# Attention inside a feed-forward pass: units of attention taken in pairs per visit to the tensor engine, PSUM banks dealt out anew, global scores in one piece, one order list for the whole program

## The chip, the cores and the metric

The kernel runs on one core of one Trainium2 chip. The metric is the device time of one execution, in microseconds; the median of three runs of the kernel before is 951.62 (951.41 to 951.68). Engines are named as in the profile: PE is the tensor engine's matmul, PEld its weight load, DVE the vector engine, ACT the scalar engine, POOL GpSimd, and SP the queue that issues most DMAs.

## The reference

Local and global attention feed a layer norm and a feed-forward network; float32 throughout.

```python
# q_l, k_l, v_l: (8 batches, 8 heads, 512, 64); q_g, k_g, v_g: (8, 8, 32, 64)
s_g = scale * q_g @ concat(k_g, k_l).T            # 32 global rows see all 544 keys
out_g = softmax(s_g) @ concat(v_g, v_l)
s_ll = where(|i - j| <= 32, scale * q_l @ k_l.T, -1e9)
s_l = concat(scale * q_l @ k_g.T, s_ll)           # a local row sees 32 global keys and a window
out_l = softmax(s_l) @ concat(v_g, v_l)
x = concat(out_g, out_l)  -> (8, 544, 512)        # heads side by side
xn = (x - mean) / sqrt(var + 1e-6) * g_ln
out = x + relu(xn @ w_ch1) @ w_ch2                # 512 -> 2048 -> 512
```

## The kernel before

**Feed-forward network.** The 4,352 rows are cut into nine chunks: eight local ones (c0 to c7) of four row tiles (512 rows) and a global one (c8) of two. A chunk runs through 16 column blocks f of the hidden layer. `Ffn.first` (L643) makes 12 matmuls of 128x512 into one PSUM bank, `ph`: the low part of the weight times the high part of x, high times low, high times high, four of each. `high` (L656) writes `hh`, the rectified block, with ACT; `low` (L662) writes `hl`, the remainder, with DVE. `second` (L669) makes three matmuls for each row tile into the banks `acc0` to `acc3`. The order on PE is first(f+1), then second(f), so that ACT and DVE have the time of second(f-1) and first(f+1) to make hh and hl of f. There are two `ph` banks (`ps_h`, `bufs=2`), which alternate.

**Attention.** The next chunk's attention is made between these matmuls, in visits of PE to it. A local unit (`Local`, L310) is 256 rows of two heads: `score` (L334) makes 16 matmuls on 64x32 tiles, 128 columns each, into halves of two banks; DVE's `lowest` (L357, four pairs of instructions) scales, masks and takes the row extreme; ACT's `exp` (L370) follows four times; `transposes` (L396) makes 16 DVE transposes into `pt` (for the first 16 units PE transposes them, `turn`, L387); `sums` (L404) makes 16 matmuls on 128x32 tiles, 64 columns each, in the free half of a score bank; `scale` (L427) writes x. There are 64 local units, eight of them ahead of the first chunk's network. The other 56 have a visit each (`visit`, L806), which scores one unit and sums the one before it.

A global unit (L550) is four batches' 32 global rows of two heads: scores in two halves of 272 columns (`score_global`, L470), in two visits, then eight PE transposes (`transpose_global`, L512, in a third), then in the next unit's second visit 40 matmuls of sums (`value_global`, L523), 32 of them in the 128x32 tiling and 8 for the last 32 keys in a 32x32 one. There are eight, all in c7. Their keys `gk` and values `gv` have one buffer each, so a unit's keys are loaded when the scores of the unit before are done (L579), and its values when that unit's sums are.

**What sets the order.** PSUM has eight banks: four `acc`, two `ph`, two `att` (taken in turn for scores, sums and transposes). The first chunk and all ahead of it are ordered by `Plan` (L53): operations with an engine, an estimated cost, a key and what they wait for, given out one by one to the engine that can begin soonest, and, among those that can begin there, the lowest key. In the first chunk the weights are also split into high and low parts (`Split`, L206), by DVE and ACT. From c1 on the order is that in which `ffn` (L694) and `visit` are written, and the constants `PLACES` (L32) say between which matmul groups the visits lie. Each engine executes its instructions in that order.

Of the kernel before, what the change touches and what calls it, by code (L numbers as in the profile page):

```python
# [19 lines left out]
P = 128  # L20
# [11 lines left out]
PLACES = {7: (1, 3.4), 9: (0, 3.5)}  # L32
# [14 lines left out]
SPREAD = 10.0  # L47
# [5 lines left out]
class Plan:  # L53
# [13 lines left out]
    def emit(self):  # L67
        free = dict.fromkeys(self.waiting, 0.0)
        wire, landed = 0.0, []
        while self.count:  # L70
            best = None
            for e, ops in self.waiting.items():
                can = [(max(free[e], t), o) for o in ops if (t := o.ready()) is not None]
                if not can:
                    continue
                if e == "SP" and len(landed) >= IN_FLIGHT:
                    can = [(max(t, landed[-IN_FLIGHT]), o) for t, o in can]
                first = min(t for t, _ in can) + PATIENCE
                t, _, o = min(
                    ((t, o.key, o) for t, o in can if t <= first), key=lambda x: (x[1], x[0])  # L80
                )
                if best is None or t < best[0]:
                    best = t, e, o
            t, e, o = best
            self.waiting[e].remove(o)
            self.count -= 1
            free[e] = o.end = t + o.cost
            if o.size:
                wire = max(wire, o.end) + o.size / WIRE
                landed.append(wire + LANDING)  # L90
                o.late = landed[-1] - o.end
            o.run()


class Operation:
    def __init__(self, engine, cost, key, run, after, behind, late, size):
        self.engine, self.cost, self.key, self.run = engine, cost, key, run
        self.after = [a for x in after for a in (x if isinstance(x, (list, tuple)) else [x]) if a]
        self.behind, self.late, self.size, self.end = behind, late, size, None

    def ready(self):
        t = 0.0
        if self.behind:
            if self.behind.end is None:
                return None
            t = self.behind.end
        for a in self.after:
            if a.end is None:
                return None
# [5 lines left out]
def attention_ffn_kernel(  # L115
# [15 lines left out]
    SA = gk.shape[4]  # L131
# [14 lines left out]
    ps_h = ctx.enter_context(tc.tile_pool(name="ps_h", bufs=2, space=bass.MemoryType.PSUM))  # L146
    ps_a = ctx.enter_context(tc.tile_pool(name="ps_a", bufs=2, space=bass.MemoryType.PSUM))
# [137 lines left out]
    def norm(x, js):  # L285

        n = Norm(x, js)
        for j in js:
            n.stats(j)
        for j in js:  # L290
            n.join(j)
        n.root()
        n.shift()

        def apply():
            for j in js:
                n.apply(j)
                yield

        return apply()  # L300

    def att(name):
        return ps_a.tile([P, 512], F32, name=name, tag="att")
# [6 lines left out]
    class Local:  # L310


        def __init__(self, b, hp, half, alone, on_pe):
# [3 lines left out]
            self.next = None  # L317

        def load(self, part=None):

            if part != 1:
                if self.alone:
                    shape, tag = [P, 2 * (KT * P + DM)], UNITS[units.index(self)]
                    u = wpool.tile(shape, F32, name="u", tag=tag)
                else:
                    u = self.ap.tile([P, eu.shape[4]], F32, name="u", bufs=2)
                self.u = u
                self.e = u[:, :21 * WIN]
                self.v = u[:, 21 * WIN:eu.shape[4]].rearrange("p (w d) -> p w d", w=8)
            ends = (0, 21 * WIN, eu.shape[4])  # L330
            c0, c1 = ends[::2] if part is None else ends[part:part + 2]
            nc.sync.dma_start(self.u[:, c0:c1], eu[self.at][:, c0:c1])

        def score(self, banks):  # L334
            self.mn = small.tile([P, 4], F32, name="mn")
            self.sm = small.tile([P, 4], F32, name="sm")
            self.p = self.ap.tile([P, 4, P], F32, name="p", bufs=3)
            sc = self.sc = [bank("sc") for bank in banks]
            self.free = sc[1][:, 2 * P:]
# [40 lines left out]
        def scores(self):  # L380
            self.score([att, att])
            yield
            for c in range(4):
                self.lowest(c)
                self.exp(c)

        def turn(self, bank):  # L387
            self.tp = bank("tp")
# [7 lines left out]
        def transposes(self):  # L396
            self.pt = self.ap.tile([P, 4, P], F32, name="pt", bufs=2)
            for g in range(4):
                gp = slice(g * WIN, (g + 1) * WIN)
                for r in range(4):  # L400
                    rp = slice(r * WIN, (r + 1) * WIN)
                    nc.vector.transpose(out=self.pt[rp, :, gp], in_=self.p[gp, :, rp])  # L402
# [17 lines left out]
        def total(self):  # L420
            self.ri = small.tile([P, 4], F32, name="ri")
# [14 lines left out]
        def values(self, pv=None):  # L436
            self.sums(att("pv") if pv is None else pv)
            self.total()
            self.inverse()
            self.scale()  # L440
            if self.next and self.next.next:
                self.next.next.load()

# [5 lines left out]
        def finish(self):  # L449
            if self.at[1] == HP - 1:  # L450
                for j in range(2):
                    self.store(j)
                return norm(self.x, range(2))
            return ()

    def load_global_keys(ap, bg, hp):
        kr = ap.tile([P, BG, SA], F32, name="gk")
        qr = ap.tile([P, BG, SG], F32, name="gq", bufs=2)
        nc.sync.dma_start(qr, gq[bg, hp])
        nc.sync.dma_start(kr, gk[bg, hp])  # L460
        return qr, kr

    def load_global_values(ap, bg, hp):
        vr = ap.tile([P, BG, 4, P], F32, name="gv")
        vt = ap.tile([P, P], F32, name="gvt")
        nc.sync.dma_start(vr, gv[bg, hp])
        nc.sync.dma_start(vt, gt[bg, hp])
        return vr, vt

    def score_global(ap, qr, kr, out):  # L470
        p = ap.tile([P, 2, SA], F32, name="gp")
        mn = small.tile([P, 4], F32, name="mn")
        sm = small.tile([P, 4], F32, name="sm")
        for part in range(2):
            c0, c1 = part * SA // 2, (part + 1) * SA // 2
            sc = [ps_a.tile([P, 512], F32, name="sc", tag="att") for _ in range(2)]
            out[:] = p, sm, sc[1][:, c1 - c0:]
            for i in range(BG):
                for h in range(2):
                    nc.tensor.matmul(  # L480
                        sc[h][i * SG:(i + 1) * SG, :c1 - c0],
                        qr[h * D:(h + 1) * D, i, :],
                        kr[h * D:(h + 1) * D, i, c0:c1],
# [5 lines left out]
            yield  # L489
            for h in range(2):  # L490
                nc.vector.tensor_scalar(
                    p[:, h, c0:c1],
                    sc[h][:, :c1 - c0],
                    -QSCALE,
                    BIG if part == 0 else mn[:, 2 * h:2 * h + 1],
                    ALU.mult,
                    ALU.min,
                    accum_out=mn[:, 2 * h + part:2 * h + part + 1],
                )
            if part == 0:  # L500
                yield
        for h in range(2):
            nc.scalar.activation(
                p[:, h, :],
                p[:, h, :],
                AF.Exp,
                bias=mn[:, 2 * h + 1:2 * h + 2],
                scale=-1.0,
                accum_out=sm[:, h:h + 1],
            )  # L510

    def transpose_global(ap, p):  # L512
        pt = ap.tile([P, 2, 4, P], F32, name="gpt")
        tail = ap.tile([P, 2, SG], F32, name="gpt_tail")
        for h in range(2):
            t0 = ps_a.tile([P, 512], F32, name="t0", tag="att")
            for c in range(4):
                nc.tensor.transpose(t0[:, c * P:(c + 1) * P], p[:, h, c * P:(c + 1) * P], ident)  # L518
            nc.vector.transpose(out=tail[:, h, :], in_=p[:, h, 512:SA])
            nc.scalar.copy(pt[:, h], t0.rearrange("p (c q) -> p c q", c=4))  # L520
        return pt, tail

    def value_global(hp, pt, tail, vr, vt, sm, x, pv):  # L523
        if pv is None:
            pv = ps_a.tile([P, 512], F32, name="pv", tag="att")
        for h, cs in enumerate(((0, 1, 2, 3, 4), (4, 0, 1, 2, 3))):
            hd = slice(h * D, (h + 1) * D)
            for c in cs:
                for i in range(BG):
# [751 lines left out]
```

## Time and profile before

| | us |
|---|---|
| median of 3 runs | 951.62 (951.41 to 951.68) |
| profiled execution | 950.43 |
| its span in the trace | 948.6 |
| outside the span | 1.8 |
| PE busy | 919.4 (97%) |
| DVE busy | 573.2 (60%) |
| ACT busy | 316.8 (33%) |

PE is busy for nearly the whole span, and the chain of work that ended last runs on PE for 87% of it; PE's idle time is 29 us in all, and most of it lies ahead of the first chunk's network. The busy share is a mean over stages, so what a piece of work takes is read from the stage it lies in. The rows further down give stages and pieces: a local chunk's network with the next chunk's attention in it takes 103 us, and c7 with the global attention 128.

### The profile page before, as it was taken

To read this page: it belongs to the slowest core of one execution; us is meant where nothing else is said; L and a number is where in the kernel's file an instruction comes from. 1 tells how busy PE (TensorE), PEld (TensorE's weight loads), DVE (VectorE), ACT (ScalarE), POOL (GpSimd) and SP (SyncE) were. 2 spreads that over 40 slices of the span, in tenths; PEclk is the share of its full clock that TensorE was granted. 3 is DMA by queue.
4 is the path that set the end of the run, shared out by engine and by line. 5 is a ranking of instruction groups with operands and counts; after the bars stand their busy time and mean duration, and the time that the engine had idled before them with its cause. 6 is when DMAs were issued, how large, how long until landed. Compare 5 with 4: busy or idle time off the path is not lost.

```text
span 948.6 us, 21082 instructions
## 1 busy us (share of the span) xinstructions
PE 919.4 (97%) x8616; PEld 716.0 (75%) x8616; DVE 573.2 (60%) x1885; ACT 316.8 (33%) x842; POOL 48.4 (5%) x150
## 2 busy tenths in 40 slices
PE   5699999999999999999999999999999999999997
PEld 3477777777777787777777777778777777777896
DVE  4799987766577647766776647664776442222311
ACT  5788843232223222322323232223232123222210
POOL 4111010000000000000000000000000000000000
PEclk9699999999999999999999999999999999999999
DMA  8766643324223223323332422323322425353300
GB/s 355 286 247 234 221 168 118 97 75 141 82 75 97 79 99 119 103 95 114 119 96 75 139 84 75 97 75 104 120 97 74 164 95 196 114 191 145 101 23 23
DMA packets 31873, 118.81 MB, mean 125 GB/s; under 512 B 4256, under 2 KB 6304, under 8 KB 27680
## 3 DMA queue, kind: packets, MB, share of 16 engines
q1 hardware_dynamic: 31776, 117.46, 35.7%
q8 instruction: 68, 1.11, 0.5%
q14 instruction: 29, 0.24, 0.1%
HBM read 99.62 MB, written 17.83 MB: 124 GB/s over the span
## 4 chain that ended last, share of the span: by engine, by line
PE 87%; DVE 5%; DMA 2%; issue 2%; ACT 2%; POOL 1%; SPq 0%; ACTq 0%; POOLq 0%; DVEq 0%
PE acc L676 40%; PE ph L651 36%; PE sc L347 3%; DVE pt L402 3%; PE sc L410 3%; DMA gk<-in_gk 2%; PE t L610 2%; PE sc L531 1%; ACT p L371 1%; PE sc L480 1%; PE tp L390 1%; DVE ob L688 1%; PE t L518 0%; POOL mask L184 0%; DVE hl L664 0%
## 5 line engine op out<-in xcount | busy, mean ns | idle before, releaser
L676 PE MATMUL acc<-w,hh 128*128 128x512 f32 x1088 | 341.9, 395 | 0.0
L651 PE MATMUL ph<-xh,w 128*128 128x512 f32 (+1 forms) x1216 | 309.9, 382 | 0.0
L402 DVE STREAM_TRANSPOSE pt<-p 32x128 f32<-32x128 f32 x768 | 232.2, 302 | 38.9 <-ACT p L371 27.0
L651 PEld LDWEIGHTS ph<-xh,w 128*128 128x128 f32 x1216 | 214.7, 188 | 49.1 <-issue 2.2
L676 PEld LDWEIGHTS acc<-w,hh 128*128 128x128 f32 x1088 | 205.1, 188 | 45.3
L664 DVE SCALAR_TENSOR_TENSOR hl<-ph,hh 128x512 fp32r<-128x512 f32 (+1 forms) x144 | 93.2, 650 | 231.7 <-ACT hh L660 231.5
L676 PE MATMUL acc<-w,hl 128*128 128x512 f32 x544 | 222.0, 408 | 0.9 <-DVE hl L664 0.6
L660 ACT ACTIVATE hh<-ph 128x512 fp32r<-128x512 f32 (+1 forms) x144 | 82.5, 573 | 384.3 <-PE ph L651 384.2
L651 PE MATMUL ph<-xl,w 128*128 128x512 f32 x512 | 141.4, 398 | 0.0
L371 ACT ACTIVATE p<-p,mn 128x128 f32<-128x128 f32 x256 | 100.2, 393 | 108.4 <-DVE mn L359 108.2
L676 PEld LDWEIGHTS acc<-w,hl 128*128 128x128 f32 x544 | 102.2, 188 | 25.8 <-DVE hl L664 2.7
L651 PEld LDWEIGHTS ph<-xl,w 128*128 128x128 f32 x512 | 96.1, 189 | 23.7
L359 DVE CUSTOM_DVE_ANT_0 p<-sc,mask 128x128 f32<-128x128 f32 x256 | 62.5, 285 | 31.7 <-PE sc L347 31.3
L347 PE MATMUL sc<-u 64*32 64x128 f32 x2048 | 46.2, 286 | 8.8 <-DMA u<-in_eu 4.5
L422 POOL TENSOR_SCALAR ri<-sm 128x4 f32<-128x4 f32 x64 | 19.6, 307 | 636.4 <-ACT p L371 636.1
L347 PEld LDWEIGHTS sc<-u 64*32 64x32 f32 x2048 | 27.4, 110 | 31.7 <-issue 24.5
L371 ACT ACTIVATION_READ_ACCUMULATOR p<-p,mn 128x1 f32 x256 | 48.0, 187 | 0.0
L274 ACT ACTIVATE x<-x,rs 128x512 f32<-128x512 f32 x32 | 24.4, 808 | 51.1 <-DVE rs L268 50.1
L410 PE MATMUL sc<-u,pt 128*32 128x64 f32 x1760 | 37.4, 222 | 0.9 <-DVE pt L402 0.9
L410 PEld LDWEIGHTS sc<-u,pt 128*32 128x32 f32 x1760 | 27.7, 109 | 12.6 <-issue 10.7
L614 ACT ACTIVATE xh<-t,g_sb 128x512 fp32r<-128x512 f32 (+1 forms) x40 | 24.8, 625 | 16.0 <-PE t L610 15.8
L618 DVE SCALAR_TENSOR_TENSOR xl<-t,g_sb,xh 128x512 fp32r<-128x512 f32 (+1 forms) x36 | 24.5, 688 | 8.8 <-ACT xh L614 8.8
(66 smaller groups left out, 458.3 us busy)
## 6 DMA issues: line engine op xcount, KB each, us to landing
u<-in_eu SPq DMA_DIRECT2D x63, 848.0 KB, 5.2
raw<-in_wd SPq DMA_DIRECT2D x16, 1024.0 KB, 4.8
gk<-in_gk SPq DMA_DIRECT2D x8, 1088.0 KB, 5.9
xs<-x SPq DMA_DIRECT2D x32, 256.0 KB, 6.0
ob<-xs SPq DMA_DIRECT2D x32, 256.0 KB, 6.1
out<-ob SPq DMA_DIRECT2D x32, 256.0 KB, 2.2
gv<-in_gv SPq DMA_DIRECT2D x8, 1024.0 KB, 5.1
u<-in_eu SPq DMA_DIRECT2D x1, 512.0 KB, 3.8
```

The lines of the kernel that those rows point to most:

```text
L274: nc.scalar.activation((self.x if to is None else to)[:, j, :], self.x[:, j, :], AF.Identity, bias=self.rs[:, 1, j:j + 1], scale=self.rs[: ...
L347: nc.tensor.matmul(sc[h][gp, qb * P:(qb + 1) * P], self.e[hd, w * WIN:(w + 1) * WIN], self.e[hd, k0 * WIN:(k0 + 4) * WIN], start=True, sto ...
L359: nc.vector.tensor_tensor_reduce(out=self.p[:, c], in0=self.sc[h][:, qb * P:(qb + 1) * P], in1=masks[self.at[2], qb], scale=-QSCALE, scala ...
L371: nc.scalar.activation(self.p[:, c], self.p[:, c], AF.Exp, bias=self.mn[:, c:c + 1], scale=-1.0, accum_out=self.sm[:, c:c + 1],)
L402: nc.vector.transpose(out=self.pt[rp, :, gp], in_=self.p[gp, :, rp])
L410: nc.tensor.matmul(pv[gp, qb * P + h * D:qb * P + h * D + D], self.pt[:, 2 * h + qb, gp], self.v[:, 4 * qb + g, h * D:(h + 1) * D], start= ...
L614: nc.scalar.activation(hi, t[:, :hi.shape[1]], AF.Copy, scale=g_sb[:, kt:kt + 1])
L618: nc.vector.scalar_tensor_tensor(lo, t[:, :hi.shape[1]], g_sb[:, kt:kt + 1], f32(hi), ALU.mult, ALU.subtract)
L651: nc.tensor.matmul(self.ph[f][:, :self.n], w[:, kt, :], xx[kt][:, :self.n], start=begins and kt == 0, stop=ends and kt == KT - 1,)
L660: nc.scalar.activation(hh[:, :self.n], self.ph[f][:, :self.n], AF.Relu)
L664: nc.vector.scalar_tensor_tensor(hl[:, :self.n], self.ph[f][:, :self.n], 0.0, f32(hh[:, :self.n]), ALU.max, ALU.subtract,)
L676: nc.tensor.matmul(self.acc[t], a[:, ts], w, start=(f == 0 and i == 0), stop=(f == NF - 1 and i == 2),)
```

## The change

- **Pairs.** A visit scores two local units and sums the two before them: 28 visits, four in a chunk (five in c0, the first of them with scores alone, ahead of the first chunk's first product). The pair's scores fill both halves of the banks `att0` and `att1`; the sums have a bank of their own, `att2`.
- **Banks.** One bank `ph` instead of two, so that first(f+1) waits until hl(f) is written; three `att` banks with names instead of two in turn. c8, whose blocks are half as wide, alternates `ph` and `att0`. The chunks' sums always use `acc0` to `acc3`.
- **Global units.** Scores of 512 columns at once, and the last 32 keys as eight matmuls of 32 columns into `att2`; sums in the 128x32 tiling throughout, the last keys with a zero-padded tile `lasts`. gq and gk are 32 columns longer for that (their last columns are put once more beside them, for the other head). Of the transposes one head's are made by DVE (16 instructions), the other's by PE (4). The visits lie at the places `GLOBAL` of c7 (place 2f is behind first(f), 2f+1 behind second(f-1)); the first unit's scores are made in c6, which has pairs at places 0, 7 and 14, the last pair's sums at 21 and the global scores at 27.
- **Loads.** A local unit's keys and values are loaded in two pieces with buffers of their own.
- **Order.** `Plan` orders the whole program, all engines. hh, hl and the visits have lower keys (by `URGENT`), a unit's 16 transposes are operations of their own with higher keys (by `SLACK`), and the visits follow each other 20 us apart in c0 (`SPREAD`).

```diff
-PLACES = {7: (1, 3.4), 9: (0, 3.5)}
-SPREAD = 10.0
+SPREAD = 20.0
+SLACK = 14.0
+URGENT = 30.0
+GLOBAL = (0, 4, 8, 11, 14, 17, 20, 24)
+PAIR = 7
+FIRST = 27
...
-    ps_h = ctx.enter_context(tc.tile_pool(name="ps_h", bufs=2, space=bass.MemoryType.PSUM))
-    ps_a = ctx.enter_context(tc.tile_pool(name="ps_a", bufs=2, space=bass.MemoryType.PSUM))
+    ps_h = ctx.enter_context(tc.tile_pool(name="ps_h", bufs=1, space=bass.MemoryType.PSUM))
+    ps_a = ctx.enter_context(tc.tile_pool(name="ps_a", bufs=1, space=bass.MemoryType.PSUM))
...
+    def att(k, name):
+        return ps_a.tile([P, 512], F32, name=name, tag=f"att{k}")
...
-        def transposes(self):
-            self.pt = self.ap.tile([P, 4, P], F32, name="pt", bufs=2)
-            for g in range(4):
-                gp = slice(g * WIN, (g + 1) * WIN)
-                for r in range(4):
-                    rp = slice(r * WIN, (r + 1) * WIN)
-                    nc.vector.transpose(out=self.pt[rp, :, gp], in_=self.p[gp, :, rp])
+        def transposes(self, g, r):
+            if g == r == 0:
+                self.pt = self.ap.tile([P, 4, P], F32, name="pt", bufs=2)
+            gp, rp = (slice(k * WIN, (k + 1) * WIN) for k in (g, r))
+            nc.vector.transpose(out=self.pt[rp, :, gp], in_=self.p[gp, :, rp])
...
+                    nc.tensor.matmul(
+                        sc[h][i * SG:(i + 1) * SG, :512],
+                        self.q[hd, i, :SG],
+                        self.k[hd, i, :512],
...
+                    nc.tensor.matmul(
+                        last[h][i * SG:(i + 1) * SG, :SG],
+                        self.q[:D, i, h * SG:(h + 1) * SG],
+                        self.k[:D, i, 512 + h * SG:512 + (h + 1) * SG],
...
-                self.ph[f] = ps_h.tile([P, 512], F32, name="ph")
+                self.ph[f] = att(0, "ph") if self.nt == 2 and f % 2 else ps_h.tile([P, 512], F32, name="ph")
...
+            def go():
+                sc = [att(k, "sc") for k in range(2)] if us else None
+                pv = att(2, "pv") if prev or not locals_ else None
+                for j, u in enumerate(us):
+                    if locals_:
+                        u.score([b[:, 256 * j:256 * j + 256] for b in sc])
+                    else:
+                        u.score(sc, [pv[:, 32 * h:32 * h + 32] for h in range(2)])
+                for j, u in enumerate(prev):
+                    into(u)
+                    u.sums(pv[:, 256 * j:256 * j + 256] if locals_ else pv[:, 256:384])
...
+            v.key -= URGENT
+            for u in us:
+                load_part(u, 1, key + 0.5, v)
+            for u in nxt:
+                load_part(u, 0, key + 0.6, v)
...
+                                waits = [hl.get((c, f - 1)) if f else hl.get((c - 1, NF - 1))]
...
+                    hh[c, f] = op("ACT", 0.59 if wide else 0.38, key - URGENT, lambda f=f, box=box: box[0].high(f),
+                                  end, second.get((c, f - 2, nt - 1)))
+                    hl[c, f] = op("DVE", 0.66 if wide else 0.39, key - URGENT, lambda f=f, box=box: box[0].low(f),
+                                  hh[c, f])
```

On PE, at the start of the first chunk's network (`t` is the last transpose of x, `ph` a first product, `sc` a local score), there stood:

```order
L610 MATMUL t<-ident,x 128x128 x8
L651 MATMUL ph<-xh_598,w 128x512 x2
L651 MATMUL ph<-xh_656,w 128x512 x2
L651 MATMUL ph<-xl_599,w 128x512 x2
L651 MATMUL ph<-xl_657,w 128x512 x2
L651 MATMUL ph<-xh_598,w 128x512 x2
L651 MATMUL ph<-xh_656,w 128x512 x2
L347 MATMUL sc<-u 32x128 x16
L651 MATMUL ph<-xh_598,w 128x512 x2
```

and now stands:

```order
L589 MATMUL t<-ident,x 128x128 x8
L350 MATMUL sc<-u_e 32x128 x32
L619 MATMUL ph<-xh_592,w 128x512 x2
L619 MATMUL ph<-xh_650,w 128x512 x2
L619 MATMUL ph<-xl_593,w 128x512 x2
L619 MATMUL ph<-xl_651,w 128x512 x2
L619 MATMUL ph<-xh_592,w 128x512 x2
L619 MATMUL ph<-xh_650,w 128x512 x2
L619 MATMUL ph<-xh_592,w 128x512 x2
```

The scores moved from behind the first of the first products to ahead of it, and are two units' instead of one's.

On PE, in c7, one global unit's scores and the sums of the one before (`gpt` the transposed weights, `gpt_tail` and `lasts` those of the last 32 keys) were:

```order
L480 MATMUL sc<-gk,gq 32x272 x8
L651 MATMUL ph<-xh_8365,w 128x512 x2
L651 MATMUL ph<-xh_8387,w 128x512 x2
L480 MATMUL sc<-gk,gq 32x272 x8
L531 MATMUL sc<-gv,gpt 32x64 x16
L531 MATMUL sc<-gvt,gpt_tail 32x64 x8
L531 MATMUL sc<-gv,gpt 32x64 x16
L651 MATMUL ph<-xl_8366,w 128x512 x2
```

and are:

```order
L463 MATMUL sc<-gk,gq 32x512 x8
L474 MATMUL pv<-gk,gq 32x32 x8
L538 MATMUL pv<-gv,gpt 32x64 x16
L538 MATMUL pv<-gvt,lasts 32x64 x4
L538 MATMUL pv<-gv,gpt 32x64 x16
L538 MATMUL pv<-gvt,lasts 32x64 x4
L644 MATMUL acc<-w,hl 128x512
```

Two visits became one, with eight small matmuls more; a visit of eight transposes elsewhere became one of four.

On DVE, behind a local visit in a middle chunk (`ISA` is `lowest`, `hl` the network's remainder), there stood:

```order
L359 ISA p,mn<-sc,mask_116 128x128
L359 ISA mn 128x1
L402 STREAM_TRANSPOSE pt<-p 32x4x32 x16
L425 RECIPROCAL ri<-ri 128x4
L664 SCALAR_TENSOR_TENSOR hl<-ph,hh 128x512 x2
L359 ISA p,mn<-sc,mask_107 128x128
```

and now stands:

```order
L362 ISA p,mn<-sc,mask_168 128x128
L362 ISA mn 128x1
L396 STREAM_TRANSPOSE pt<-p 32x4x32 x2
L419 RECIPROCAL ri<-ri 128x4 x2
L396 STREAM_TRANSPOSE pt<-p 32x4x32 x4
L632 SCALAR_TENSOR_TENSOR hl<-ph,hh 128x512
L396 STREAM_TRANSPOSE pt<-p 32x4x32 x16
L632 SCALAR_TENSOR_TENSOR hl<-ph,hh 128x512
L396 STREAM_TRANSPOSE pt<-p 32x4x32 x10
L632 SCALAR_TENSOR_TENSOR hl<-ph,hh 128x512 x2
```

The 16 transposes of a unit were one piece ahead of two hl; the 32 of a pair are in pieces of 2, 4, 16 and 10 with hl between them.

## Rows read from the trace of the kernel before

**Rows 1.** The page's first part: busy us (share of the span) of each engine.

```profile
PE 919.4 (97%) x8616; PEld 716.0 (75%) x8616; DVE 573.2 (60%) x1885; ACT 316.8 (33%) x842; POOL 48.4 (5%) x150
```

**Rows 2.** Windows: us, busy by engine, PEclk, DMA share, GB/s; c0's start, c4, c7.

```profile
42.30:56.00 13.70, 13.70 (x86) 10.61 (x85) 13.52 (x24) 11.08 (x21) 0.93 (x1) 0.91 0.46 161
56.00:70.00 14.00, 14.00 (x180) 10.72 (x179) 13.64 (x33) 12.78 (x26) 1.42 (x1) 1.00 0.69 241
...
357.30:460.40 103.10, 102.68 (x914) 80.32 (x912) 68.73 (x243) 28.59 (x88) 3.69 (x12) 1.00 0.30 99
769.10:897.10 128.00, 124.37 (x1354) 91.68 (x1354) 37.47 (x127) 34.52 (x70) 3.37 (x12) 1.00 0.41 148
```

**Rows 3.** PE's timeline in c5: start, us, line, operation; one block f without a visit.

```profile
494.66 0.39 PE L676 MATMUL acc<-w,hl 128*128 128x512 f32 x1
...
500.26 0.40 PE L676 MATMUL acc<-w,hl 128*128 128x512 f32 x1
```

**Rows 4.** PE's timeline in c5: a visit and the network's matmul behind it.

```profile
480.80 0.67 PE L347 MATMUL sc<-u 64*32 64x128 f32 x32
481.40 0.65 PE L410 MATMUL sc<-u,pt 128*32 128x64 f32 x32
481.98 0.50 PE L676 MATMUL acc<-w,hl 128*128 128x512 f32 x1
```

**Rows 5.** PE's timeline in c5: sums that wait for pt (in brackets: idle, releaser).

```profile
468.14 0.31 PE L410 MATMUL sc<-u,pt 128*32 128x64 f32 x6
468.62 0.63 PE L410 MATMUL sc<-u,pt 128*32 128x64 f32 x26 [0.17 <-DVE pt L402]
469.41 0.50 PE L676 MATMUL acc<-w,hl 128*128 128x512 f32 x1
```

**Rows 6.** PE's timeline in c7: the two visits of a global unit.

```profile
823.57 0.69 PE L480 MATMUL sc<-gk,gq 64*32 64x272 f32 x16
824.19 1.20 PE L651 MATMUL ph<-xh,w 128*128 128x512 f32 x4
825.32 0.69 PE L480 MATMUL sc<-gk,gq 64*32 64x272 f32 x16
825.94 0.65 PE L531 MATMUL sc<-gv,gpt 128*32 128x64 f32 x32
826.52 0.43 PE L531 MATMUL sc<-gvt,gpt_tail 32*32 32x64 f32 x16
826.88 0.65 PE L531 MATMUL sc<-gv,gpt 128*32 128x64 f32 x32
827.47 0.49 PE L651 MATMUL ph<-xl,w 128*128 128x512 f32 x1
```

**Rows 7.** PE's timeline in c7: a unit's transposes; scores that wait for keys.

```profile
790.21 1.04 PE L518 MATMUL t<-ident,gp 128*128 128x128 f32 x8
791.00 1.18 PE L651 MATMUL ph<-xh,w 128*128 128x512 f32 x4
...
795.06 0.69 PE L480 MATMUL sc<-gk,gq 64*32 64x272 f32 x16 [1.01 <-DMA gk<-in_gk]
```

**Rows 8.** The chain that ended last: start, us, what; those keys' transfer.

```profile
786.94 7.98 DMA gk<-in_gk
```

**Rows 9.** DVE's timeline in c5: hl behind a unit's transposes.

```profile
496.65 2.53 DVE L402 STREAM_TRANSPOSE pt<-p 32x128 f32<-32x128 f32 x8
...
499.31 0.66 DVE L664 SCALAR_TENSOR_TENSOR hl<-ph,hh 128x512 fp32r<-128x512 f32 x1
```

**Rows 10.** Timeline, PE and DVE, at the first chunk's start.

```profile
42.31 2.06 PE L651 MATMUL ph<-xh,w 128*128 128x512 f32 x4
44.16 1.41 PE L651 MATMUL ph<-xl,w 128*128 128x512 f32 x4
...
47.03 1.20 PE L651 MATMUL ph<-xh,w 128*128 128x512 f32 x4
...
48.85 0.69 DVE L664 SCALAR_TENSOR_TENSOR hl<-ph,hh 128x512 fp32r<-128x512 f32 x1
```

## What the change is expected to do

> **What bounds the kernel now.** First the page's busy shares: PE is busy for 919.4 of 948.6 us, DVE for 573.2 [rows 1]. Then windows by stage: in c4 PE is busy for 102.68 of 103.10 us with DVE at 68.73, in c7 for 124.37 of 128.00; only at the first chunk's start does another engine run as full as PE, DVE with 13.52 of 13.70 us and then 13.64 of 14.00 [rows 2]. So nearly everywhere a microsecond of PE's work is a microsecond of the span, and PE's timeline prices it. One block f of 24 matmuls takes 500.26 − 494.66 = 5.60 us, 0.233 each, 89.6 for the 16 blocks of a chunk [rows 3].
>
> A visit has 480.80 to 481.40 for the scores, 0.60, and to 481.98 for the sums, 0.58 [rows 4]. What entering and leaving it cost on top is read in c7: four first products stand between two visits and should take 0.93, but 825.32 − 824.19 = 1.13 pass [rows 6], so 0.20. A visit takes 0.60 + 0.58 + 0.20 = 1.38 from the network. The period of c4 closes with that: 89.6, eight visits 11.0, one wait of 0.69 (below), and the four groups of x transposes for the next chunk at 0.44 each, 1.8 (half of the eight-transpose visit below): 103.1, as the window has it [rows 2].
>
> **Pairs.** They remove 28 of 56 entries; the units' matmuls stay. How much of a visit is fixed? 16 records of the global sums take 826.88 − 826.52 = 0.36, 32 take 826.52 − 825.94 = 0.58 [rows 6], so 16 more cost 0.22 and 0.14 are there whatever their number. With 0.14 taken for the scores as well, 0.46 of their 0.60 are work; 16 records of 272 columns, 6% more columns, should then take 0.63 and took 825.94 − 825.32 = 0.62 [rows 6]. Fixed are 0.20 + 0.14 + 0.14 = 0.48, and a pair's visit takes 2.28 instead of 2.76. 28 × 0.48 = 13.4 us. Should each unit's run begin anew inside a visit, only the 0.20 goes: 28 × 0.20 = 5.6. I take 13.4, since those two rows show runs that grow by their slope. The Trainium skill ("TensorEngine Tiling (Array Packing)", Key Properties) says that a change of the tiling mode drains TensorE, but a change of tile alone does not; two units in one mode would then share the drain, as rows 6 have it for 16 and 32 records, and by the rule the sum is 13.4 too, where a drain at every unit would make it 5.6. In c0 PE's own transposes of eight units are grouped in twos, four entries less, some 0.4.
>
> **Global units.** Before: first visit 0.20 + 0.62 = 0.82; second visit 0.20 and 827.47 − 825.32 = 2.15, together 2.35 [rows 6]; transposes 791.00 − 790.21 = 0.79 [rows 7] and half an entry, 0.88. That is 4.05 each. After: one entry 0.20; scores of 16 records of 512 columns, by the slope 0.14 + 0.90 = 1.04; the last keys' small matmuls, 16 records in a run of their own, 0.15; sums of 80 records in one mode 0.14 + 5 × 0.22 = 1.24; four transposes 0.44: 3.07. Eight times 0.97 is 7.8 us. The small matmuls are not in the trace; between nothing (hidden behind the long ones) and 0.36 (the 16-record row) I take 0.15, near the fixed part, since they stream 32 columns only; the ends move the sum by +1.7 and −1.2. The eight units' half sets of transposes that go to DVE, 16 short instructions each, fall where it has room: 37.47 of 128 us busy [rows 2].
>
> **Waits that go.** In c5 the sums start at 468.14 and the network resumes at 469.41, 1.27 instead of 0.58: 0.69 of waiting for pt [rows 5]: visits are two blocks apart, and DVE's 16 transposes end late in them. The trace has one such wait in each of c1 to c6: 4.1. With pairs 4 × 5.60 + 0.44 = 22.8 us of network lie between visits. In that time DVE has for a pair 32 transposes at 2.53 / 8 = 0.316 [rows 9], 10.1, some 3.5 of `lowest` and scale, and four hl at 0.66, 2.6: 16.2, so pt should be there and I count no wait. In c7 128.0 pass [rows 2], against 89.6 + 8 × 4.05 + 0.9 for the halved x transposes = 122.9: 5.1 of waits, the largest like the 1.01 for keys at 795.06 [rows 7], whose transfer took 7.98 us from 786.94 [rows 8]. After, the closest visits are three places apart, 8.4 us of network and a turn, 8.8, against that transfer of 8, now 6% longer and issued behind the values. I leave 2 us of waiting there; zero and 8 (1 per unit) are the ends. So 4.1 + 5.1 − 2.0 = 7.2 us go. What is late next is the network's own handoff, below.
>
> **One bank for first products.** first(f+1) now starts only when hl(f) is written. Undisturbed that costs nothing: hl takes 0.66 [rows 9] and hh, ahead of it on ACT, about as long, with two handovers some 1.6 by my estimate; second(f−1) covers 2.8, half a block [rows 3]. Cover is gone where hl stands behind a unit's transposes. Before, it did: first(f) ended at 494.66 [rows 3] and hl at 499.31 + 0.66 = 499.97 [rows 9], 5.3 us later, which two banks absorbed. The new order has pieces of transposes between hl's, 16 at most (5.1 us, with one hl 5.7 in a block of 5.6), so hl is late by tenths and the 1.2 of slack takes it. I count nothing for c1 to c7; the other end is the second rival.
>
> **The first chunk.** There the cover is thin. A pair's scores come ahead of the first product, at the lower of TensorE's clock levels: four matmuls took 44.16 − 42.31 = 1.85 there [rows 10], twice the 0.93, and the granted clock is 0.91 over the window [rows 2]. More than that, DVE splits weights all the time, and hl(0) ended at 48.85 + 0.69 = 49.54, while the second first product had begun at 47.03 [rows 10]. It must now wait: 2.5 us, less 0.1 of the visit that was between. For the next block I take half of that with the surplus of the pair's work moved ahead, 1.0, and 1.0 for the rest while DVE is full: +4.4. Ends: 0 (hl has a lower key than the splits now, and is put ahead of some) and five blocks of these 28 us at 2.5 each, 12.5.
>
> **Sum.** On the profiled execution's 950.43: −13.4 −0.4 −7.8 −7.2 +4.4 = 926.0. The median of the runs shown lies 1.2 above the profiled execution, so 927 for the median. The parts outside (ahead of 42 us, the tail behind c8) keep their instructions, and longer lists cost the engines nothing. SP gets 56 more DMA issues of a third of a microsecond, hidden: no rival hangs on it.
>
> **Rivals.**
> - *Nothing merges*: each unit's run inside a visit pays its fixed part. For it: the merged run of 64 records is in no row. Against: the slope in rows 6. The time: 927 + 7.8 = 935.
> - *The late handoff* (the slower side): hl comes late for each pair, as it did behind each block of 16 transposes before, and with one bank PE stands still. Price: 5.3 − 2.8 = 2.5 at least once for each of the 24 pairs in c1 to c6, 60 us: 987. From 24.7 / 24 = 1.0 us a pair it is slower than before. For it: the row of before, and DVE's queue is in order, so one late exp holds the transposes and hl behind them. Against: hl stands between pieces, and DVE is busy for two thirds only in the middle chunks [rows 2]. The Trainium skill ("TensorEngine Tiling (Array Packing)", PSUM Bottleneck) says that tiling makes the products faster but not the emptying of the banks, which may become the limit; here the rows show 5.3 us of emptying in before, and by that rule the sum would be this rival's 987.
> - *The first chunk is worse*: DVE, at 98%, holds each of its first five blocks, 12.5 instead of 4.4: 935.
> - *It doesn't do what it says in c7*: keys and values still come late, 1 us a unit: 927 + 6 = 933.
>
> **Chances.** Forecast 0.62, with its own range 921 to 932; nothing merges 0.11; first chunk worse 0.10; c7 0.08; late handoff 0.06, of which 0.05 slower; something less than 921 0.03. The range for 8 in 10 reaches from 919, where first chunk and c7's waits cost nothing (−4.4, −2.0, and a little for the small matmuls), to 939, where two of the smaller rivals meet in part. Within 0.2%, which is what a measurement of this kernel can tell from no change, lie 949.7 to 953.5; only a late handoff of the right size falls there: 0.02. Slower 0.05, faster 0.93.
>
> **What would show it.** In the changed profile: a pair's visit of 2.3 us between network matmuls (2.6 or more: nothing merges); PE busy lower by some 21; c1 to c5 at 89.6 + 4 × 2.28 + 1.8 = 100.5 each; PE's idle time ahead of first products with hl as releaser near zero in c1 to c6 and 4 to 5 us in c0; c7 near 116. Wrong it is if first products show idle time for hl in each chunk, if DVE's busy share in the middle chunks nears PE's, or if global scores still wait for gk by a microsecond each.

## The result, and the profile after

The changed kernel takes 922.07 us (median of 4 runs, 921.82 to 923.49); the kernel before took 951.51 beside it (950.01 to 951.68). The ratio is 0.970, with a 95% interval of 0.968 to 0.971: 29 us faster. The forecast was 927, so 5 us of gain came on top; the direction, the mechanism and most of the terms held.

The page of the changed kernel, its first part and, of the fourth, the chain that ended last by engine:

```profile
PE 895.0 (97%) x8584; PEld 716.1 (78%) x8584; DVE 597.2 (65%) x2029; ACT 312.2 (34%) x834; POOL 46.6 (5%) x151
...
PE 94%; DVE 0%; issue 0%
```

PE's busy time fell by 24.4 us against [rows 1] and the span by 26.9 (948.6 to 921.7): nearly all of the gain lies in PE's busy time. That is not work alone, since busy time holds part of the waits: of the 0.69 us lost in [rows 5] the trace records 0.17 as idle. The chain is now PE's for 94%.

Windows of the changed kernel, in the columns of [rows 2]: the first chunk's start, a middle chunk, and c7:

```profile
42.50:56.00 13.50, 11.30 (x99) 8.83 (x98) 12.79 (x31) 10.30 (x23) 0.00 (x0) 0.82 0.85 320
...
353.75:454.40 100.65, 100.65 (x914) 80.74 (x913) 65.51 (x243) 28.58 (x88) 3.66 (x12) 1.00 0.31 102
...
757.02:870.12 113.10, 113.10 (x1286) 88.05 (x1285) 72.33 (x242) 28.41 (x57) 3.12 (x11) 1.00 0.45 163
```

From first product to first product, c1 to c5 take 100.65 each instead of 103.08, c7 113.10 instead of 127.93, and in both PE is busy for the whole window: no wait is left there. Between c0's first product and c8's, PE stands still only in the first chunk, for 2.20 of 13.50 us. The ledger by stage, each from one first product to the next chunk's:

| stage | before | after | change |
|---|---|---|---|
| up to c0's first product | 42.31 | 44.17 | +1.86 |
| c0 | 110.20 | 108.27 | −1.93 |
| c1 to c5, together | 515.41 | 503.26 | −12.15 |
| c6 | 101.22 | 101.32 | +0.10 |
| c7 | 127.93 | 113.10 | −14.83 |
| c8 and the tail | 51.6 | 51.6 | 0.0 |

c6 has the first global scores in it now, which were in c7's part before, and so shows no gain of its own.

PE's timeline of the changed kernel in c3: a pair's visit between the network's matmuls.

```profile
377.55 1.09 PE L619 MATMUL ph<-xh,w 128*128 128x512 f32 x4
378.57 1.16 PE L350 MATMUL sc<-u_e 64*32 64x128 f32 x64
379.65 1.10 PE L404 MATMUL pv<-u_v,pt 128*32 128x64 f32 x64
380.69 0.50 PE L644 MATMUL acc<-w,hl 128*128 128x512 f32 x1
```

Scores 1.08, sums 1.04, with 0.20 around them 2.32, against 1.38 for one unit [rows 4]; the forecast said 2.28. The wait for pt that [rows 5] shows is gone.

DVE's timeline behind that visit:

```profile
387.28 0.69 DVE L632 SCALAR_TENSOR_TENSOR hl<-ph,hh 128x512 fp32r<-128x512 f32 x1 [1.10 <-ACT hh L628]
388.00 4.17 DVE L396 STREAM_TRANSPOSE pt<-p 32x128 f32<-32x128 f32 x16
392.88 0.69 DVE L632 SCALAR_TENSOR_TENSOR hl<-ph,hh 128x512 fp32r<-128x512 f32 x1 [0.71 <-ACT hh L628]
```

hl does not stand behind the transposes as in [rows 9]; it waits for hh (the 0.71 in brackets), and ends 1.5 to 1.9 us after the last first product throughout c1 to c7. Even 16 transposes between two hl end before the next is due.

PE's timeline in c7: a global unit's scores with the sums of the one before, and a turn.

```profile
773.43 1.09 PE L463 MATMUL sc<-gk,gq 64*32 64x512 f32 x16
...
786.94 1.09 PE L463 MATMUL sc<-gk,gq 64*32 64x512 f32 x16
787.83 0.33 PE L474 MATMUL pv<-gk,gq 64*32 64x32 f32 x16
788.08 0.65 PE L538 MATMUL pv<-gv,gpt 128*32 128x64 f32 x32
788.55 0.29 PE L538 MATMUL pv<-gvt,lasts 128*32 128x64 f32 x8
...
789.33 0.50 PE L644 MATMUL acc<-w,hl 128*128 128x512 f32 x1
...
794.35 0.60 PE L511 MATMUL tp<-ident,gp 128*128 128x128 f32 x4
794.70 0.48 PE L644 MATMUL acc<-w,hl 128*128 128x512 f32 x1
```

The visit is 789.33 − 786.94 = 2.39 and 0.20, the turn 0.35 and 0.09: 3.03 for a unit, where [rows 6, 7] gave 4.05 and the forecast said 3.07. Its parts were less well guessed: the 512-column scores took 0.89 (forecast 1.04), the 16 small ones 0.25 (0.15). No scores of c7 wait for keys any more. Before, PE's idle time in c7 was this, from the waits of the kernel before (us in total, times, longest):

```profile
PE sc L480 <- DMA gk<-in_gk: 2.1, 3, 1.0
PE sc L480 <- DVE gp L491: 1.5, 2, 1.2
```

So three waits were for keys. The other two, 1.5 us, were for DVE, which was still reading the banks of a unit's first half of the scores when PE came with the second half; with the scores in one piece there is no second half.

PE's timeline at the first chunk's start, for [rows 10]:

```profile
42.49 1.75 PE L350 MATMUL sc<-u_e 64*32 64x128 f32 x64
44.17 1.20 PE L619 MATMUL ph<-xh,w 128*128 128x512 f32 x4
...
49.44 1.21 PE L619 MATMUL ph<-xh,w 128*128 128x512 f32 x4 [2.20 <-DVE hl L632]
50.49 1.71 PE L619 MATMUL ph<-xl,w 128*128 128x512 f32 x4
51.99 1.91 PE L619 MATMUL ph<-xh,w 128*128 128x512 f32 x4
53.70 0.60 PE L644 MATMUL acc<-w,hl 128*128 128x512 f32 x1
```

The pair's scores stand ahead of the first product, and the second first product waits 2.20 us for hl, at 49.44 instead of 47.03. Behind that wait its twelve matmuls took 53.70 − 49.44 = 4.26 us instead of 2.80: the granted clock, 0.82 over the window, fell once more to the lower level. The kernel before paid for that level too, in its first product (1.85 us for four matmuls instead of 0.93 [rows 10]).

### The profile page after: what moved, and what is told of

Same layout as the page of the kernel before. It is cut to its first block, busy times and chain, and to the rows that moved or that the text cites. A ratio compares the mean times of both kernels' runs of the same rounds, so it can differ in the third digit from the quotient of the medians.

```text
span 921.7 us, 21075 instructions
## 1 busy us (share of the span) xinstructions
PE 895.0 (97%) x8584; PEld 716.1 (78%) x8584; DVE 597.2 (65%) x2029; ACT 312.2 (34%) x834; POOL 46.6 (5%) x151
## 4 chain that ended last, share of the span: by engine, by line
PE 94%; DVE 0%; issue 0%
PE acc L644 42%; PE ph L619 42%; PE sc L350 3%; PE pv L404 3%; PE t L589 1%; PE pv L538 1%; PE sc L463 1%; PE tp L511 0%; PE tp L386 0%; DVE tmp L247 0%; DVE w L261 0%; PE pv L474 0%; DVE ob L656 0%; DVE hl L632 0%; DVE tmp L243 0%
## 5 line engine op out<-in xcount | busy, mean ns | idle before, releaser
L632 DVE SCALAR_TENSOR_TENSOR hl<-ph,hh 128x512 fp32r<-128x512 f32 (+1 forms) x144 | 95.2, 661 | 224.4 <-ACT hh L628 223.7
L396 DVE STREAM_TRANSPOSE pt<-p 32x128 f32<-32x128 f32 x768 | 214.2, 292 | 15.7 <-ACT p L374 6.3
L362 DVE CUSTOM_DVE_ANT_0 p<-sc,mask 128x128 f32<-128x128 f32 x256 | 59.2, 285 | 14.3 <-PE sc L350 13.8
L416 POOL TENSOR_SCALAR ri<-sm 128x4 f32<-128x4 f32 x64 | 17.4, 271 | 651.6 <-ACT p L374 651.2
L521 DVE STREAM_TRANSPOSE gpt<-gp 32x128 f32<-32x128 f32 x128 | 38.6, 302 | 2.0
L350 PEld LDWEIGHTS sc<-u_e 64*32 64x32 f32 x1792 | 25.5, 107 | 10.2 <-issue 9.1
L423 DVE TENSOR_TENSOR x<-pv,ri 128x256 f32<-128x256 f32 x64 | 24.8, 419 | 13.2 <-PE pv L404 13.2
L350 PE MATMUL sc<-u_e 64*32 64x128 f32 x1792 | 33.0, 278 | 0.0
L404 PE MATMUL pv<-u_v,pt 128*32 128x64 f32 x1792 | 30.8, 221 | 0.0
L404 PEld LDWEIGHTS pv<-u_v,pt 128*32 128x32 f32 x1792 | 26.3, 110 | 5.7 <-issue 5.7
```

The lines of the kernel that those rows point to most:

```text
L350: nc.tensor.matmul(sc[h][gp, qb * P:(qb + 1) * P], self.e[hd, w * WIN:(w + 1) * WIN], self.e[hd, k0 * WIN:(k0 + 4) * WIN], start=True, sto ...
L362: nc.vector.tensor_tensor_reduce(out=self.p[:, c], in0=self.sc[h][:, qb * P:(qb + 1) * P], in1=masks[self.at[2], qb], scale=-QSCALE, scala ...
L404: nc.tensor.matmul(pv[gp, qb * P + h * D:qb * P + h * D + D], self.pt[:, 2 * h + qb, gp], self.v[:, 4 * qb + g, h * D:(h + 1) * D], start= ...
L423: nc.vector.tensor_tensor(self.x[:, :, hp * P:(hp + 1) * P].rearrange("p q (h d) -> p q h d", h=2), self.pv[:, :256].rearrange("p (q h d) ...
L521: nc.vector.transpose(out=self.pt[rp, 0, :, ip], in_=p[ip, :, r])
L632: nc.vector.scalar_tensor_tensor(hl[:, :self.n], self.ph[f][:, :self.n], 0.0, f32(hh[:, :self.n]), ALU.max, ALU.subtract,)
```

## The experiments

**One unit per visit.** All else as changed.

```diff
-        pairs = [tuple(phases[0][n:n + 2]) for n in range(n0, len(phases[0]), 2)]
+        pairs = [(u,) for u in phases[0][n0:]]
```

and visits at half the distance (`SPREAD / 2`, places `4 * k` and, in c6, `3 * k`).

> One unit per visit again, 56 visits instead of 28, everything else as in the changed kernel (one bank for first products, one order list, whole global scores). Theory (a visit has a fixed part that the pair shares, 2 x 1.38 against the 2.31 us that a pair's visit took): 27 to 28 more visits at 0.45 to 0.48, 12 to 13 us more, 934 to 936, a visit of 1.38 us in the trace. Rival (nothing merges, only entry and exit are shared): 28 x 0.20, 928. Rival (the order, not the pairing, gave the gain): below 925.

Measured: 936.74 (936.30 to 937.71), 14.7 more than the changed kernel's 922.07 and 0.7 above the range expected. A visit on PE's timeline in c4, and the window of c3:

```profile
463.42 0.67 PE L350 MATMUL sc<-u_e 64*32 64x128 f32 x32
464.01 0.65 PE L404 MATMUL pv<-u_v,pt 128*32 128x64 f32 x32
464.96 1.20 PE L619 MATMUL ph<-xh,w 128*128 128x512 f32 x4 [0.29 <-DVE hl L632]
```

```profile
357.81:460.52 102.71, 102.42 (x913) 80.33 (x912) 68.52 (x243) 29.02 (x89) 3.67 (x12) 1.00 0.31 100
```

A chunk takes 2.06 more, 0.51 for each of four pairs undone: 0.44 of PE's work (busy 102.42 against 100.65) and 0.07 of waits, 0.29 a chunk, which only single units have (in the last row above, for hl). The rival with 928 falls, and so does the one that gave the order alone the gain: pairs are worth half of the 29 us.

**Scores and sums in turn inside a visit.** `go()` scores and sums unit by unit:

```diff
-                for j, u in enumerate(us):
-                    ...
-                for j, u in enumerate(prev):
+                for j in range(max(len(us), len(prev))):
+                    for u in us[j:j + 1]:
+                        ...
+                    for u in prev[j:j + 1]:
```

> Pairs as in the changed kernel, but inside a visit the order is scores of the first unit, sums of the first, scores of the second, sums of the second: four runs of matmuls in two tilings instead of two runs. Theory (each run has 0.14 us that don't depend on its length): 2 x 0.14 more in each of 27 visits, 7.6 us, 929 to 930, a visit of 2.6 us. Rival (the fixed part is all in entering and leaving the network's tiling): no change, 922.

Measured: 929.83 (927.55 to 930.42), ratio to the kernel before 0.978 (0.977 to 0.979). The same visit of c3:

```profile
379.12 0.67 PE L350 MATMUL sc<-u_e 64*32 64x128 f32 x32
379.72 0.65 PE L404 MATMUL pv<-u_v,pt 128*32 128x64 f32 x32
380.31 0.67 PE L350 MATMUL sc<-u_e 64*32 64x128 f32 x32
380.90 0.65 PE L404 MATMUL pv<-u_v,pt 128*32 128x64 f32 x32
381.49 0.50 PE L644 MATMUL acc<-w,hl 128*128 128x512 f32 x1
```

No matmul was added or enlarged, and 381.49 − 379.12 = 2.37 stands against 2.12 before (380.69 − 378.57). So two runs more cost 0.25, 0.125 each, and the chunk's four visits 1.00 (101.65 against 100.65); the forecast had 0.14. The rule of the Trainium skill ("TensorEngine Tiling (Array Packing)", Key Properties), that a change of the tiling mode drains TensorE and a change of tile does not, agrees with it: what is paid for is the change.

**Another bank for the second first product.** In c0 alone it goes into `att2`.

```diff
-                self.ph[f] = att(0, "ph") if self.nt == 2 and f % 2 else ps_h.tile([P, 512], F32, name="ph")
+                self.ph[f] = att(0, "ph") if self.nt == 2 and f % 2 else att(2, "ph") if self.early and f == 1 else ps_h.tile([P, 512], F32, name="ph")
...
+                            if c == 0 and f in (1, 2):
+                                waits = [half_of[1]["low"]] if f == 1 else [hl[0, 0]]
```

> In the first chunk alone, the second first product goes into the bank att2, which is free there, so that it needn't wait for hl of the first; the third waits for hl of the first instead of the second. Theory (PE stood still for 2.4 us at 47.07 to 49.44 for hl, and its clock fell to the lower level at 50.7 after that idle time): 2.4 us less for the wait and up to 1.5 us less for the clock, 918 to 920. Rival (DVE, full with the split of the weights, is the bound of the first chunk's start): the wait comes back ahead of the next blocks, for hl or for weights, 922.

Measured: 920.89 (919.83 to 921.36). Its start:

```profile
44.95 2.07 PE L620 MATMUL ph<-xh,w 128*128 128x512 f32 x4
46.82 1.33 PE L620 MATMUL ph<-xl,w 128*128 128x512 f32 x4
47.99 2.03 PE L620 MATMUL ph<-xh,w 128*128 128x512 f32 x8
```

The last row has eight matmuls in one piece: the wait is gone, and it did not come back, since PE is busy for all of c0's 105.30 us. But the time is above the 918 to 920 expected, and 1.2 us against runs that were not made beside it settles nothing; so the changed kernel was run again beside the next version.

**The changed kernel again.**

> The changed kernel itself once more, on the chip of the three runs beside it. Theory (its profiled execution, 923.49, was slowed by 1.5 us because TensorE's clock fell a second time, at 50.7 us, after PE had waited for hl): 921.5 to 922.5 in the median, and the second dip need not be there in the profile; from c1's first product on, the stages of 100.65, 101.3 and 113.1 us repeat within 0.1. Rival (the stages differ from execution to execution): other stage times.

Measured: 922.27 (921.58 to 923.07). The stages repeat: 100.65 and 113.09. Its start:

```profile
44.76 2.07 PE L619 MATMUL ph<-xh,w 128*128 128x512 f32 x4
...
47.72 1.10 PE L619 MATMUL ph<-xh,w 128*128 128x512 f32 x4
50.23 1.20 PE L619 MATMUL ph<-xh,w 128*128 128x512 f32 x4 [1.41 <-DVE hl L632]
```

Here the first product itself ran at the lower level (2.07 for four), and the second did not (1.20, as at 47.03 in [rows 10]). So where the clock is low in these 20 us differs between executions of one program, the length of the wait too (1.41 here, 2.20 in the first profile), and c0 with them (106.93 and 108.27); the second fall is no fixed price of the wait.

**That bank, and the x transposes in two visits.** As e3_bank, and each of `turn_next`'s operations makes two groups of four transposes.

> The bank att2 for the second first product, as in the run before, and the x transposes for the next chunk in two visits of eight instead of four of four. Theory: the bank gives the wait for hl, 1.7 us; two visits fewer save 0.09 of leaving each, in eight chunks 1.4 us; together 3 below the changed kernel on the same chip. Rival (the second bank gave nothing, and the x transposes' copies come too late when two share a visit): no faster than the changed kernel.

Measured: 919.74 (919.50 to 922.35), 2.5 below the changed kernel on the same chip; the ratios to the kernel before are 0.967 (0.965 to 0.969) and 0.969 (0.967 to 0.971), which overlap, so this is a likely gain rather than a certain one. Windows of c0 and c3, and on PE's timeline one visit of x transposes:

```profile
44.30:148.55 104.25, 104.25 (x953) 84.21 (x945) 97.16 (x221) 77.47 (x154) 8.36 (x14) 1.00 0.60 217
349.90:450.58 100.68, 100.68 (x913) 80.83 (x912) 65.16 (x243) 28.45 (x88) 3.67 (x12) 1.00 0.30 102
```

```profile
342.53 1.04 PE L589 MATMUL t<-ident,x 128*128 128x128 f32 x8
343.32 0.48 PE L645 MATMUL acc<-w,hl 128*128 128x512 f32 x1
```

In c0 PE is busy for all of 104.25 us, 2.7 less than beside it. The bank's part of that is the wait of 1.41. Another 1.1 is the clock: beside it the first eight matmuls ran at the lower level, 47.72 − 44.76 = 2.96 us instead of 1.87, and that differs between executions. The grouped transposes gave nothing, 100.68 against 100.65: eight take 0.79, four took 0.35 (346.41 to 346.76 in the changed kernel), so what two visits less save, the longer run takes. That half of the expectation failed.

**hl written twice, and three times.** In the chunks of four row tiles `low` repeats its instruction, and the order list counts its time twice or three times:

```diff
-            nc.vector.scalar_tensor_tensor(
+            for _ in range(2 if self.nt == 4 else 1):     # and 3
+                nc.vector.scalar_tensor_tensor(
```

> DVE writes hl twice in the chunks of four row tiles, 0.68 us more ahead of the next first product, 10.9 us more of DVE's work a chunk. Theory (hl ends 1.5 to 1.8 us after the last first product, and PE comes back to that bank 2.8 us after it, so 1.0 is to spare): c1 to c7 unchanged, c0 1 to 3 us longer, 923 to 925. Rival (the handoff of the one bank is on the path that sets the end): 0.68 for 112 blocks, 76 us, 998.

> DVE writes hl three times in the chunks of four row tiles. Theory (twice left 0.5 us of slack, 2.30 against 2.79; a third one takes 0.69 more and hl then ends 2.99 after the last first product): 0.2 us of waiting in each block that has no visit behind its first product, some 12 in a chunk, 2.4 to 3 us a chunk in c1 to c7, 20 in all, and in c0 as much as DVE's 11 us of added work there, 945 to 960. Rival (what costs is DVE's total work, which is 85 of 100 us then and fits): no more than in e7_hl2, 929 to 935.

Measured: 929.12 (928.73 to 930.89) and 985.73 (985.27 to 986.31). Windows of c0 and c3 of the one with two, then the window of c3 and DVE's and PE's timeline in it of the one with three:

```profile
44.60:155.04 110.44, 106.42 (x952) 84.27 (x945) 106.33 (x235) 77.36 (x153) 7.91 (x14) 0.99 0.56 203
357.06:457.86 100.80, 100.73 (x913) 80.73 (x912) 74.54 (x259) 28.71 (x88) 3.67 (x12) 1.00 0.31 102
```

```profile
380.05:486.38 106.33, 103.34 (x913) 79.95 (x912) 85.01 (x275) 28.50 (x88) 3.67 (x12) 1.00 0.29 96
```

```profile
421.59 2.14 DVE L633 SCALAR_TENSOR_TENSOR hl<-ph,hh 128x512 fp32r<-128x512 f32 x3 [0.40 <-ACT hh L628]
```

```profile
423.79 1.20 PE L619 MATMUL ph<-xh,w 128*128 128x512 f32 x4
```

Twice costs a middle chunk 0.15 us, though DVE has 9 more to do in it: hl then ends 2.30 after the last first product, and PE comes back at 2.80. Three times, hl ends at 423.73 and the first product starts 0.06 behind it; the chunk takes 106.33, 5.7 more, with DVE still at 85.01. So the handoff has about 1.0 us to spare and then lies wholly on the path, and DVE's total is not what costs. The sizes were missed on both: 923 to 925 and 945 to 960 were expected. Of the 6.9 us of the first, 3.5 are c0 (110.44 against 106.93), where PE now stands still for 4.0, and the rest is 0.6 to 0.7 each in c1, c7 and the tail, and pieces. Of the second, c0 took 14 more (120.66) and c7 11 more (124.11); in c7 hl ends up to 3.9 after the last first product.

**hl behind all of a pair's transposes.** In c1 to c6 hh and hl lose `URGENT` (the line of hl stands here, that of hh is changed alike), and the transposes go ahead of them.

```diff
-                        o.append(op("DVE", 0.31, key + SLACK, lambda u=u, k=k: u.transposes(*divmod(k, 4)),
+                        o.append(op("DVE", 0.31, key - (20 if units.index(u) >= 24 else -SLACK), lambda u=u, k=k: u.transposes(*divmod(k, 4)),
...
-                    hl[c, f] = op("DVE", 0.66 if wide else 0.39, key - URGENT, lambda f=f, box=box: box[0].low(f),
+                    hl[c, f] = op("DVE", 0.66 if wide else 0.39, key - (0 if 0 < c < last_chunk - 1 else URGENT), lambda f=f, box=box: box[0].low(f),
```

> In c1 to c6 the order list gives hh and hl no lower key and the pair's 32 transposes a lower one, so that on DVE one hl stands behind all 32 (order: 32 transposes, one hl, three hl); banks, pairs and the rest as in the changed kernel. Theory (with one bank an hl that comes later than 2.8 us after the last first product stops PE; the changed kernel is fast since hl stands between pieces of transposes): 32 x 0.32 = 10 us of transposes ahead of one hl in each of some 23 visits, less the 1.2 of slack, 7 to 9 us each, 160 to 200 us, 1,080 to 1,120, with PE idle for hl ahead of first products. Rival (the slack absorbs it, or other hl come earlier): 922 to 930.

Measured: 1098.98 (1098.12 to 1099.84). In c3, DVE's timeline, PE's, and the window of the chunk:

```profile
403.34 10.10 DVE L396 STREAM_TRANSPOSE pt<-p 32x128 f32<-32x128 f32 x32 [1.05 <-ACT p L374]
...
413.63 0.66 DVE L632 SCALAR_TENSOR_TENSOR hl<-ph,hh 128x512 fp32r<-128x512 f32 x1
```

```profile
414.35 2.08 PE L619 MATMUL ph<-xh,w 128*128 128x512 f32 x4 [8.35 <-DVE hl L632]
...
419.63 0.45 PE L644 MATMUL acc<-w,hl 128*128 128x512 f32 x1
```

```profile
395.13:529.59 134.46, 109.12 (x914) 86.04 (x912) 68.39 (x243) 28.35 (x88) 3.67 (x12) 0.91 0.23 76
```

The late handoff is real: 33.8 us a chunk, 8.5 a pair, from the order of the same instructions. Part of it is the clock, 0.91 over the chunk: behind a wait of 8.35 us twelve matmuls took 419.63 − 414.35 = 5.3 us instead of 2.8.

**All global transposes on PE.** `turn` makes both heads' eight, the 16 DVE transposes go.

> Global units: both heads' 128x128 transposes on PE (eight, as in the kernel before), none of them on DVE; the rest as in the changed kernel. Theory (PE sets c7's time): four more transposes, 0.35 us by their own row, for eight units, 2.8 us more, 924.9. Rival (the DVE transposes delay the visits): less than 922. Rival (the visits come closer to each other, 9.8 us of network between two scores instead of 10.5, and the keys come late): 1 us a unit on top, 932.

Measured: 925.90 (925.05 to 926.36), 1.0 above the forecast. c7 takes 116.23 instead of 113.10, c6 0.48 more; 0.45 a unit, since eight transposes took 0.79 and not twice 0.35. DVE's busy time in c7 falls from 72.33 to 39.37 us and gives nothing back: PE sets c7's time.

**Global visits nearer to each other.** As e4_gpe, with

```diff
-GLOBAL = (0, 4, 8, 11, 14, 17, 20, 24)
+GLOBAL = (0, 3, 6, 9, 12, 15, 18, 21)
...
-            u.size = 1.2, 1.15
+            u.size = 0.3, 0.3
```

> Global units: all transposes on PE as in e4_gpe, and visits as near to each other as 7 to 9 us of network (9.8 to 10.5 before), by other places and by loads that the order list takes for short. Theory (in the changed kernel the visits lie just behind the keys' landing, 9.7 us after the visit before, and so nothing waits; nearer visits must wait for gk): 1 to 2 us of waiting for gk in six visits on top of e4_gpe's 925.9, 932 to 937. Rival (the merged visit alone took the wait away): 925.9.

Measured: 930.64 (929.08 to 932.08). PE's timeline in c7:

```profile
771.58 1.09 PE L463 MATMUL sc<-gk,gq 64*32 64x512 f32 x16 [1.38 <-DMA gk<-in_gk]
...
795.05 1.09 PE L463 MATMUL sc<-gk,gq 64*32 64x512 f32 x16 [1.51 <-DMA gk<-in_gk]
...
831.57 1.09 PE L463 MATMUL sc<-gk,gq 64*32 64x512 f32 x16 [0.88 <-DMA gk<-in_gk]
```

The waits for keys are back, in three of six visits and 3.8 us in all (c7 takes 120.20 against 116.23), which leaves the time under the 932 to 937 expected. So merging the visits does not take them away by itself: with 13.5 us from one unit's scores to the next one's they are gone, and with 11 to 13 they come back.

## Why the prediction was right, and where it was off

*Pairs* (13.4 forecast). A pair's visit took 2.32, not 2.28: 0.44 × 28 = 12.3 by the rows, and 0.51 a pair with the waits of single units. The split of the fixed part held: 0.20 for the network's tiling, 0.125 a run. But that 0.14 was forecast is in part luck: it is the slope between 16 records and 32 [rows 6], and the 16 are on 32*32 tiles, the 32 on 128*32 ones, so these rows are not two lengths of one run. "Nothing merges" is out.

*Global units* (7.8). 4.05 − 3.03 = 1.02 each, 8.2; two errors in the parts cancelled.

*Waits* (7.2). The step that failed is the 2.0 left in c7: "after, the closest visits are three places apart, 8.4 us of network and a turn". They are not. A place is only the earliest point for a visit, and the order list puts it where its inputs are expected: scores follow each other by 13.5 us (773.43, 786.94 and on), about 11 us of which lie behind a visit's end, and gk had landed at the latest 9.7 us behind it. The prediction took the table of places for the order. When the distance was forced down, 3.8 us of waiting came. So 9.2 went, not 7.2. Nor were the 5.1 of before all like the wait for keys that was named: of PE's 3.6 us of recorded idle time in c7, keys took 2.1 and DVE 1.5.

*One bank* (nothing in c1 to c7). Right: hl ends 1.5 to 1.9 us after the last first product where 1.6 was estimated, which leaves 1.0 of slack, near the 1.2 forecast; and the late handoff, the rival on the slower side, is what the order of hl and transposes avoids: it would have cost 8.5 us a pair, more than three times the price of 2.5 that the rival was given, since 32 transposes and not 16 can stand ahead and the clock falls during the wait.

*The first chunk* (+4.4). The wait for hl of 2.5 was there: 2.20 and 1.41 in two executions. Of the other 2.0, counted for the next two blocks, hardly any wait showed; in their place stood the low clock, 1.5 us in the profiled execution, though the kernel before had some of that as well. The terms that gained come to 12.3 + 0.4 + 9.2 + 8.2 = 30.1, and 26.9 was gained, so what is left for the first chunk is +3.2.

By these terms the profiled execution came to 923.49 where 926.0 was forecast: 2.5 us, of which the waits of c7 are 2.0; that pairs gave 1.1 less than forecast and the first chunk cost 1.2 less is two errors that cancel. The other half of the miss is no mechanism: the forecast added 1.2 us from the profiled execution to the median, as before had it, and this time the profiled execution was the slowest of four, 1.4 above the median. The stages from c1 on are the same to 0.1 us in the two profiled executions, so the spread probably lies ahead of c1.

## What to carry to other kernels

Where an engine is full, count its entries as well as its work: here nearly half a microsecond was paid each time PE left the network's tiling for two runs of small matmuls, and two units behind one entry took as much off as all of the global part's rewriting. When a buffer is given up (a second bank here), measure how late its reader ends and what stands ahead of it in that engine's queue; the second bank could go only because hl was moved between the transposes. And read places from the order that comes out, not from the table that goes in.

## What the runs showed of the hardware that was not expected

By the piece, the small matmuls look alike: 64 records of 128 columns took 1.08 us and 64 of 64 columns 1.04, some 17 and 16 ns each. But the first are on 64*32 tiles and the second on 128*32 ones, which are twice as large. On the 64*32 tiles alone the time goes by the columns: 16 records of 512 columns took 0.89 us, for the same 8,192 columns as the 64 records of 128. Of the 0.19 between them, 0.125 is by the run above the change of tiling that only the short ones have behind them; so 48 more records cost under 0.1 us. The 64 records on 128*32 tiles have 4,096 columns, half as many, in about the same time: a column on the larger tiles cost about twice as much.

DVE's transposes of one shape took 10.10 / 32 = 0.316 us each in one place, 2.53 / 8 in [rows 9], and 4.17 / 16 = 0.26 in another, where single hl stood around them. What makes the difference is open.
